# Two interleaved token tiles: the left sides of the sequence transform read as weights with a step of two

## The chip, the cores and the metric

The kernel runs on one core of one Trainium2 chip. The metric is device time in microseconds (us), from runs of the whole program. All data is fp32; the matrix products run on TensorE with operands of the type fp32r, which are split into a high part and a low remainder beforehand, so that three products (high x high, high x low, low x high) stand for one.

## The reference, cut to what matters

The kernel computes a gated sum of a linear-attention block and a Fourier mixing block over 2048 tokens of width 576. The part that the change touches is the last one, the transform along the sequence:

```python
def _B_ref(x, dft_seq_re, dft_seq_im, dft_hid_re, dft_hid_im):
...
    a = jnp.einsum("bsd,ed->bse", x, dft_hid_re)
    b = jnp.einsum("bsd,ed->bse", x, dft_hid_im)
...
    y = jnp.einsum("ts,bse->bte", dft_seq_re, a) - jnp.einsum("ts,bse->bte", dft_seq_im, b)
    return y
...
x = A_x
g = _sigmoid((x * gate_w).sum(-1, keepdims=True))
a = _A_ref(x, A_wqkv, A_wo)
b = _B_ref(x, B_dft_seq_re, B_dft_seq_im, B_dft_hid_re, B_dft_hid_im)
return g * a + (1 - g) * b
```

`dft_seq_re` and `dft_seq_im` are 2048 x 2048, `a` and `b` are 2048 x 576. So two products of 2048 x 2048 by 2048 x 576 are wanted, one for the real and one for the imaginary part.

## The kernel before, in words

The program has these stages, in order of time: the keys of all token tiles, the key-value sums, the queries, the attention output, then for the real part a hidden transform (`Hidden.run`) and a sequence transform (`sequence`), and the same two stages for the imaginary part. A token tile has 128 tokens, so there are 16 of them.

**The product.** Each of the four big products of the Fourier part is done by a 2 x 2 block scheme with seven products instead of eight. For the sequence transform the left matrix (`cr` or `ci`) is cut into four quarters, and the right side (what the hidden transform left in `factors`) likewise. Out of the four quarters of the left side VectorE makes three further sums, so that seven left forms stand side by side. `PRODUCTS` says for each of the seven products which left form `l` meets which right form `f`.

**A batch.** `sequence` walks through `NP * NB` = 32 batches. A batch has one output tile pair (`j`, 8 of them) and one of the four blocks `b` of the contracted tokens. A block holds `BS` = 2 tiles of 128 contracted tokens, numbered by `k`. `Matrix.load` fetches the four quarters of a batch by one DMA on SP's queue into a tile `r` of the shape [128 partitions, 7 forms, 2, 128], forms 3 to 6. `Matrix.make` lets VectorE make forms 0 to 3 from them (L195), ScalarE round all seven to the high part `hi` (L175), and VectorE subtract to get the low part `lo` (L185). All of these operations run over whole rows of the tile and treat its columns alike.

**The matmuls.** Then come 7 products x 2 tiles `k` x 3 passes = 42 matmuls of a batch, each with its own weight load: the left form `c[x][:, l, k]` (128 partitions x 128 columns) is the stationary operand, and `factors[p](y, f)` (128 x 288) is streamed past it into one of seven banks of PSUM. The 128 columns of one left form and one `k` lie next to each other in the tile before. For both sequence transforms together this makes 2 x 32 x 42 = 2688 matmuls and as many loads, all recorded at L1133. After the fourth block of an output tile pair, ScalarE and VectorE empty the banks, mix the rows with the gate and SP's queue stores them.

**What sets the order.** The program order of SP, ScalarE, VectorE and TensorE is written out by hand (`manual_schedule`). Three batches are on their way ahead of the one that is multiplied (`m.load(n + 3)`), and the forms of the next one are made while TensorE works on the present one.

**The host side.** `_layouts` reorders the inputs before the launch. Its function `seq` brings each of the two sequence matrices into the order in which `Matrix.load` reads it: batch by batch, 128 partitions, then four quarters, two tiles `k`, 128 columns.

The two lines around which the change turns are the load of a batch and the use of its tile:

```python
nc.sync.dma_start(out=r[:, 3:7], in_=self.src[j, b])
...
nc.tensor.matmul(ps[q], c[x][:, l, k], factors[p](y, f), ...)
```

Of the kernel before, what the change touches and what calls it, by code (L numbers as in the profile page):

```python
# [14 lines left out]
P = 128  # L15
# [9 lines left out]
NP = NT // 2  # L25
BS = 2
NB = NP // BS
# [26 lines left out]
class Ring:  # L54
# [5 lines left out]
    def next(self):  # L60
        self.n += 1
        return self.at[(self.n - 1) % len(self.at)]
# [71 lines left out]
def kernel(  # L134
# [18 lines left out]
    nc = tc.nc  # L153
# [4 lines left out]
    def at(offset, shape, dtype=F, name="t"):  # L158
        count[0] += 1
        t = nc.alloc_sbuf_tensor_at(f"{name}_{count[0]}", list(shape), dtype,  # L160
                                    offset=base + offset)
        return t.ap()
# [8 lines left out]
    def bank():  # L171
        return psum.tile([P, 512], F, tag="bank", name="bank")
# [17 lines left out]
    def tick():  # L190
        while pending:
            pending.pop(0)()

    def add(dst, a, b, op=ALU.add):
        nc.vector.tensor_tensor(out=dst, in0=a, in1=b, op=op)  # L195
# [11 lines left out]
    def half(h):  # L207
        return slice(h * HALF, (h + 1) * HALF)
# [314 lines left out]
    ps = [[bank()[:, :HALF] for _ in range(2)] for _ in range(FT)]  # L523
# [163 lines left out]
    for c in range(5):  # L687
        ps = [bank(), bank()]
# [223 lines left out]
    factors, backlog = [], []  # L912
# [177 lines left out]

    mix_ring = Ring(MIX_AT, D * 4, 4)

    def sequence(m, g, src, dst, last=None, between=None):
        late, held, stores, rest_lows = [], [], [], []
        for n in range(NP * NB):
            j, b = divmod(n, NB)
            m.load(n + 3)
            if b == 0:
                ps = {k: bank()[:, :HALF] for k in PRODUCTS}
                row = {t: at(mix_ring.next(), [P, D], F, "row") for t in (j, j + NP)}  # L1100
                for t, a in row.items():
                    nc.sync.dma_start(out=a, in_=src[t])
            c = m.ready.pop(0)
            while stores:
                stores.pop(0)()
            if n == 2:
                tick()
                while rest_lows:
                    rest_lows.pop()()
            if m.raws:  # L1110
                new = m.make()
                next(new)
                next(new)
                if b < NB - 1:
                    next(new, None)
            else:
                new = iter(())
                tick()
            if n == 1:
                while backlog:  # L1120
                    backlog.pop(0)()
                rest_lows += pending[-2:]
                del pending[-2:]
            end = last is not None and j == NP - 1
            held.append((b, c))
            if end and b == NB - 2:
                continue
            for q, (l, f) in PRODUCTS.items():
                for b, c in held:
                    for k in range(BS):  # L1130
                        p = b * BS + k
                        for i, (x, y) in enumerate(TURN if n or b else FULL):
                            nc.tensor.matmul(ps[q], c[x][:, l, k], factors[p](y, f),  # L1133
                                             start=(p == 0 and i == 0),
                                             stop=(p == NP - 1 and i == 2))
            held.clear()
            if between is not None:
                between(n)
            while late:
                late.pop(0)()  # L1140
            if b < NB - 1:
                continue
            y = at(Y_AT, [P, 2, 2, HALF], F, "ys")
            c11, c12, c21, c22 = (y[:, i // 2, i % 2] for i in range(4))

            def mix(t, v, h=None, g=g, row=row, store=True, end=end):
                cs = slice(0, D) if h is None else half(h)
                a = row[t][:, cs]
                nc.vector.scalar_tensor_tensor(a, v, g[:, t:t + 1], a, op0=ALU.mult, op1=ALU.add)
                if store:  # L1150
                    stores.append(lambda: nc.sync.dma_start(out=dst[t][:, cs], in_=a))
                if store and end:
                    stores.pop()()

            nc.scalar.activation(c11, ps[1], AF.Copy)
            tick()
            add(c12, ps[6], c11, ALU.subtract)
            add(c11, ps[2], c11)
            next(new, None)
            if end:  # L1160
                mix(j, c11, 0)
                add(c21, c12, ps[7], ALU.subtract)
                add(c12, ps[5], c12)
                add(c22, c12, ps[7], ALU.subtract)
                mix(j + NP, c22, 1)
                mix(j + NP, c21, 0, store=False)
                mix(j, c12, 1, last, store=False)
                mix(j, ps[3], 1)
                mix(j + NP, ps[4], 0, last)
            else:  # L1170
                add(c21, c12, ps[7], ALU.subtract)
                add(c12, ps[5], c12)
                add(c22, c12, ps[7], ALU.subtract)
                add(c12, ps[3], c12, ALU.subtract)
                add(c21, c21, ps[4], ALU.subtract)
                late += [lambda t=t, i=i, y=y, mix=mix: mix(t, y[:, i].rearrange("p a b -> p (a b)"))
                         for i, t in enumerate((j, j + NP))]
        for f in late:
            f()
        for f in stores:  # L1180
            f()
# [11 lines left out]
    for i in range(NT):  # L1193
# [3 lines left out]
        for h in range(2):  # L1197
            ps = bank()
# [62 lines left out]
    mr.load(0)  # L1261
    first.run(mr, {1: 5, 2: 6, 6: 7}, {0: 5, 1: 6, 3: 7})
    sequence(mr, gate_n, att, mid, between=late)
    factors.clear()
    second.run(mi, {1: 5, 2: 6, 6: 7}, {0: 5, 1: 7})
    sequence(mi, gate_m, mid, [out[t * P:(t + 1) * P] for t in range(NT)], last=gate_n)
    paced.close()


def _rows(a):  # L1270

    import numpy as np

    a = np.concatenate([a, a[512:]], axis=0)
    return a.reshape(5, P, a.shape[1]).transpose(1, 0, 2)


def _layouts(inputs):
    import numpy as np

    def seq(c):


        c = c.reshape(2, NP, P, 2, NB, BS, P)
        c = np.stack([c[1, :, :, 0], c[0, :, :, 0], c[1, :, :, 1], c[0, :, :, 1]])
        return c.transpose(1, 3, 5, 0, 4, 2)

    def halves(a):

        a = a.reshape(2, HALF, -1)  # L1290
        return a[:, :2 * P].reshape(2, 2, P, -1), a[:, 2 * P:]

    def left(xt):


        main, rest = halves(xt)
        main = main.reshape(2, 2, P, 2, NP, P)
        rest = rest.reshape(2, 32, 2, 2, 4, P)
        quarters = ((1, 1), (0, 0), (1, 0), (0, 1))
        main = np.stack([main[d, :, :, h] for d, h in quarters])  # L1300
        rest = np.stack([rest[d, :, h] for d, h in quarters])
        main = main.transpose(3, 2, 0, 1, 4).reshape(NP, P, 4, 2 * P)
        rest = rest.transpose(1, 3, 0, 2, 4).reshape(1, P, 4, 2 * P)
        return np.concatenate([main, rest])

    def right(w):

        main, rest = halves(w)
        quarters = ((0, 0), (1, 0), (1, 1), (0, 1))
        cols = (slice(0, HALF), slice(HALF, D))  # L1310
        main = np.stack([main[d][:, :, cols[c]] for d, c in quarters], axis=2)
        rest = np.stack([rest[d][:, cols[c]] for d, c in quarters], axis=1)
        return main, np.concatenate([rest] * 3)

    x = inputs["A_x"][0]
    wr, wr_rest = right(inputs["B_dft_hid_re"].T)
    wi, wi_rest = right(inputs["B_dft_hid_im"].T)
    wqkv, gw = inputs["A_wqkv"], inputs["gate_w"][:, None]
    twice = np.concatenate([x, x[:, KC * P:]], axis=1)
    return {  # L1320
        "xa": _rows(x.T).reshape(P, 5, NT, P).transpose(2, 0, 1, 3),
        "xf": _rows(x.T)[:, :, :FT * P].transpose(1, 0, 2),
        "xg": twice.reshape(NT, P, 5, P).transpose(2, 1, 0, 3),
        "wk": _rows(wqkv[:, D:2 * D]),
        "wq": _rows(np.concatenate([wqkv[:, :D], gw, gw], axis=1)),
        "wv": _rows(wqkv[:, 2 * D:]),
        "wo": inputs["A_wo"],
        "xq": left(x.T),
        "wr": wr,
        "wr_rest": wr_rest,  # L1330
        "wi": wi,
        "wi_rest": wi_rest,
        "cr": seq(inputs["B_dft_seq_re"]),
        "ci": seq(inputs["B_dft_seq_im"]),
    }

# [19 lines left out]
```

## Time and profile before

| | |
|---|---|
| median of 3 runs | 724.67 us (724.57 to 725.0) |
| time of the profiled execution | 725.31 us |
| its span, first to last instruction | 723.6 us |
| granted TensorE clock, mean | 1.000 of full speed |
| mean over the span of what the DMA engines moved | 218 GB/s |

The profile shows one execution of the program. PE stands for the matmuls of TensorE and PEld for its weight loads, which overlap the matmuls; DVE is VectorE, ACT is ScalarE, POOL is GpSimd, SP issues DMAs. A row of a group gives the line of the kernel, the engine, the operation, the tiles written and read with their shapes, how many there are, the time in which at least one of them ran, and the mean duration of one in ns. The profiler models the end of a matmul, so that the durations of successive matmuls overlap; the pace of TensorE is read from the starts.

### The profile page before, as it was taken

To read this page: it belongs to the slowest core of one execution; us is meant where nothing else is said; L and a number is where in the kernel's file an instruction comes from. 1 tells how busy PE (TensorE), PEld (TensorE's weight loads), DVE (VectorE), ACT (ScalarE), POOL (GpSimd) and SP (SyncE) were. 2 spreads that over 40 slices of the span, in tenths; PEclk is the share of its full clock that TensorE was granted. 3 is DMA by queue.
4 is the path that set the end of the run, shared out by engine and by line. 5 is a ranking of instruction groups with operands and counts; after the bars stand their busy time and mean duration, and the time that the engine had idled before them with its cause. 6 is when DMAs were issued, how large, how long until landed. Compare 5 with 4: busy or idle time off the path is not lost.

```text
span 723.6 us, 13786 instructions
## 1 busy us (share of the span) xinstructions
PE 718.9 (99%) x5436; PEld 718.3 (99%) x5436; DVE 594.6 (82%) x954; ACT 331.8 (46%) x519; POOL 54.1 (7%) x94
## 2 busy tenths in 40 slices
PE   9999999999999999999999999999999999999998
PEld 9999999999999999999999999999999999999997
DVE  5699876787999828989999999857889988778884
ACT  5998445678644534453434334223535432342331
POOL 1112200050131100000010000000000000000000
PEclk9999999999999999999999999999999999999999
DMA  7388887874594699544475586889963543454440
GB/s 256 105 286 297 305 304 214 295 223 118 182 358 177 228 321 388 160 153 131 157 249 189 167 289 198 287 313 401 380 214 130 175 143 136 125 179 153 153 154 34
DMA packets 54836, 157.83 MB, mean 218 GB/s; under 512 B 6388, under 2 KB 12084, under 8 KB 53748
## 3 DMA queue, kind: packets, MB, share of 16 engines
q1 hardware_dynamic: 45716, 118.44, 48.5%
q0 software_dynamic: 8768, 38.12, 14.5%
q8 instruction: 43, 0.70, 0.4%
q10 hardware_dynamic: 288, 0.39, 0.2%
q14 instruction: 21, 0.17, 0.1%
HBM read 114.06 MB, written 41.39 MB: 215 GB/s over the span
## 4 chain that ended last, share of the span: by engine, by line
PE 93%; DVE 6%; issue 0%; ACT 0%; DVEq 0%; POOL 0%; POOLq 0%
PE bank L1133 49%; PE bank L205 18%; PE bank L979 14%; PE bank L696 8%; PE bank L532 2%; DVE qs L185 1%; DVE acc L775 1%; DVE pz L767 1%; DVE den L768 1%; PE bank L231 1%; PE bank L678 0%; DVE xb L185 0%; DVE den L772 0%; PE bank L797 0%; DVE xb L195 0%
## 5 line engine op out<-in xcount | busy, mean ns | idle before, releaser
L1133 PE MATMUL bank<-fh,c 128*128 128x288 f32 x1792 | 354.7, 294 | 0.0
L1133 PEld LDWEIGHTS bank<-fh,c 128*128 128x128 f32 x1792 | 286.7, 188 | 0.0
L1133 PE MATMUL bank<-fl,c 128*128 128x288 f32 x896 | 263.6, 294 | 0.0
L175 ACT ACTIVATE c<-craw 128x1792 fp32r<-128x1792 f32 (+1 forms) x84 | 121.3, 1447 | 169.9 <-DVE craw L195 161.2
L1133 PEld LDWEIGHTS bank<-fl,c 128*128 128x128 f32 x896 | 168.7, 188 | 0.0
L185 DVE TENSOR_TENSOR c<-craw,c 128x1792 fp32r<-128x1792 f32 (+4 forms) x86 | 141.9, 1653 | 1.5 <-ACT c L175 1.4
L195 DVE TENSOR_TENSOR craw<-craw 128x256 f32<-128x256 f32 (+1 forms) x192 | 97.9, 512 | 22.0 <-DMA craw<-in_ci_dram 13.6
L205 PE MATMUL bank<-wd,xs 128*128 128x288 f32 (+1 forms) x784 | 105.9, 295 | 0.0
L205 PEld LDWEIGHTS bank<-wd,xs 128*128 128x128 f32 x784 | 104.6, 188 | 0.0
L979 PE MATMUL bank<-wf,xf 128*128 128x288 f32 x588 | 91.1, 295 | 0.0
L979 PEld LDWEIGHTS bank<-wf,xf 128*128 128x128 f32 x588 | 83.4, 189 | 0.0
L205 PE MATMUL bank<-mw,qs 128*128 128x288 f32 x448 | 61.8, 296 | 0.1
L696 PE MATMUL bank<-pk,c 128*128 128x288 f32 x448 | 60.6, 296 | 0.0
L205 PEld LDWEIGHTS bank<-mw,qs 128*128 128x128 f32 x448 | 59.8, 188 | 0.5 <-DVE qs L185 0.4
L696 PEld LDWEIGHTS bank<-pk,c 128*128 128x128 f32 x448 | 59.7, 189 | 0.0
L370 DVE SCALAR_TENSOR_TENSOR acc<-bank,e 128x288 f32<-128x288 f32 x64 | 28.5, 452 | 17.3 <-ACT e L369 17.1
L195 DVE TENSOR_TENSOR ys<-bank,ys 128x288 f32<-128x288 f32 x63 | 28.8, 456 | 16.0 <-PE bank L1133 12.6
L185 DVE TENSOR_TENSOR fl<-fl,fh 128x864 fp32r<-128x864 f32 (+1 forms) x32 | 34.5, 1093 | 6.6 <-ACT fh L175 5.3
L175 ACT ACTIVATE fh<-fl 128x864 fp32r<-128x864 f32 (+1 forms) x32 | 29.8, 950 | 16.6 <-DVE fl L195 16.6
L195 DVE TENSOR_TENSOR fl<-bank,y 128x288 f32<-128x288 f32 x48 | 21.6, 450 | 15.8 <-PE bank L979 15.8
L979 PE MATMUL bank<-wf,xr 96*128 96x288 f32 x112 | 33.3, 298 | 0.0
L195 DVE TENSOR_TENSOR ys<-ys,bank 128x288 f32<-128x288 f32 x47 | 21.2, 450 | 12.4 <-PE bank L1133 11.8
(106 smaller groups left out, 639.6 us busy)
## 6 DMA issues: line engine op xcount, KB each, us to landing
xf<-xm SPq DMA_DIRECT2D x42, 512.0 KB, 8.4
craw<-in_cr_dram SPq DMA_DIRECT2D x32, 512.0 KB, 3.6
craw<-in_ci_dram SPq DMA_DIRECT2D x32, 512.0 KB, 3.7
xm<-xb POOLq DMA_DIRECT2D x8, 1024.0 KB, 5.8
wf<-wm SPq DMA_DIRECT2D x14, 576.0 KB, 6.2
xraw<-in_xa_dram SPq DMA_DIRECT2D x25, 320.0 KB, 3.5
xr<-xr SPq DMA_DIRECT2D x14, 448.0 KB, 8.0
xm<-xb POOLq DMA_DIRECT2D x8, 768.0 KB, 7.4
```

The lines of the kernel that those rows point to most:

```text
L175: return nc.scalar.activation(dst, src, AF.Copy, bias=bias)
L185: nc.vector.tensor_tensor(out=dst, in0=src, in1=hi, op=ALU.subtract)
L195: nc.vector.tensor_tensor(out=dst, in0=a, in1=b, op=op)
L205: nc.tensor.matmul(ps, a, b, start=(n == 0), stop=(n == len(pairs) - 1))
L231: nc.tensor.matmul(warm[:, :P], ones_f, ones_f, start=True, stop=True)
L370: nc.vector.scalar_tensor_tensor(dst, ps, 0.0, e, op0=ALU.max, op1=ALU.add)
L532: nc.tensor.matmul(ps[i][h], x[:, i_x * P:(i_x + 1) * P], wkt.row(h, j), start=(c == 0 and n == 0), stop=(c == KC and n == 1))
L696: nc.tensor.matmul(ps[h][:, :HALF], t[:, a, k], pk[s][:, b, half(h)], start=(s == 0 and n == 0), stop=(s == NT - 1 and n == len(passes) - 1))
L767: nc.vector.scalar_tensor_tensor(pz, acc[2 * k + i], EPS, zb, op0=ALU.add, op1=ALU.mult)
L768: nc.vector.tensor_reduce(out=d[:, i], in_=pz.rearrange("p (h d) -> p h d", d=DH), op=ALU.add, axis=AX.X)
L979: nc.tensor.matmul(ps, a, b, start=(start and n == 0), stop=(n == len(ops) - 1), skip_group_check=True)
L1133: nc.tensor.matmul(ps[q], c[x][:, l, k], factors[p](y, f), start=(p == 0 and i == 0), stop=(p == NP - 1 and i == 2))
```

## The change

The two tiles `k` of a batch are no longer kept one after the other. The host writes their columns in turns: column 0 of tile 0, column 0 of tile 1, column 1 of tile 0, and so on. The tile on the chip keeps its shape and its size; a row of one form still has 256 numbers. A new view `woven` picks the columns of one tile `k` out of such a row, 128 numbers of four bytes that lie eight bytes apart, and the matmul takes it as its stationary operand. DMA, sums, rounding and subtraction are written as before.

```diff
+    def woven(c, l, k):
+        return c[:, l].rearrange("p a b -> p (a b)").rearrange("p (n k) -> p k n", k=BS)[:, k]
+
     def sequence(m, g, src, dst, last=None, between=None):
...
-                            nc.tensor.matmul(ps[q], c[x][:, l, k], factors[p](y, f),
+                            nc.tensor.matmul(ps[q], woven(c[x], l, k), factors[p](y, f),
                                              start=(p == 0 and i == 0),
                                              stop=(p == NP - 1 and i == 2))
...
         c = c.reshape(2, NP, P, 2, NB, BS, P)
         c = np.stack([c[1, :, :, 0], c[0, :, :, 0], c[1, :, :, 1], c[0, :, :, 1]])
-        return c.transpose(1, 3, 5, 0, 4, 2)
+        c = c.transpose(1, 3, 5, 0, 2, 4)
+        return c.reshape(NP, NB, P, 4, BS, P)
```

## The prediction

> **What bounds the kernel now.** I read the page's first and second part, then the end of the chain of waits, then the stages one by one.
>
> ```profile
> span 723.6 us, 13786 instructions
> PE 718.9 (99%) x5436; PEld 718.3 (99%) x5436; DVE 594.6 (82%) x954; ACT 331.8 (46%) x519; POOL 54.1 (7%) x94
> PEclk9999999999999999999999999999999999999999
> PE bank L1133 49%; PE bank L205 18%; PE bank L979 14%; PE bank L696 8%; PE bank L532 2%; DVE qs L185 1%; DVE acc L775 1%; DVE pz L767 1%; DVE den L768 1%; PE bank L231 1%; PE bank L678 0%; DVE xb L185 0%; DVE den L772 0%; PE bank L797 0%; DVE xb L195 0%
> ...
> 313.66 177.16 PE bank L1133 x1344
> 490.82 52.07 PE bank L979 x392
> 542.89 174.03 PE bank L1133 x1320
> 718.41 1.39 DVE row L1149 x3
> ```
>
> TensorE is busy from end to end at a full clock, and the line of the sequence matmuls, L1133, alone is 49% of the chain. In the real sequence transform 1344 matmuls follow one another for 177.16 us, which is 131.8 ns each, with nothing in between; in the imaginary one 1320 of them take 174.03 us, again 131.8 ns. The change touches these matmuls and no others. So the question is what sets 131.8 ns: the streaming of 288 columns, or the weight load.
>
> The groups by form at L1133 can't answer it, since durations of one (294 and 188 ns) overlap:
>
> ```profile
> L1133 PE MATMUL bank<-fh,c 128*128 128x288 f32 x1792 | 354.7, 294 | 0.0
> L1133 PEld LDWEIGHTS bank<-fh,c 128*128 128x128 f32 x1792 | 286.7, 188 | 0.0
> ```
>
> The starts can. The first four rows that follow are weight loads ahead of short matmuls, elsewhere in the kernel, and show how fast loads go when they are what is waited for; the next two are matmuls with only 72 weight columns but 288 streamed ones.
>
> ```profile
> 183.07 0.80 PEld L797 LDWEIGHTS bank<-ident,acc 128*128 128x128 f32 x7
> 183.84 0.14 PEld L798 LDWEIGHTS bank<-ident,last 128*128 128x128 f32 x1
> ...
> 84.14 0.19 PEld L678 LDWEIGHTS bank<-gt,plain 128*126 128x126 f32 x1
> ...
> 84.83 0.14 PEld L678 LDWEIGHTS bank<-gt,plain 128*72 128x72 f32 x1
> ...
> 155.68 0.95 PE L205 MATMUL bank<-plain,kvb 72*72 72x288 f32 x6
> 156.47 0.30 PE L205 MATMUL bank<-wd,xs 128*128 128x288 f32 x1
> ```
>
> Seven loads of 128 columns start within 183.84 - 183.07 = 0.77 us: 110 ns each. Between 84.14 and 84.83 there are six loads of 126 columns (three at L678 and three at L681, in turns): 115 ns each. So a load occupies its path for 110 to 115 ns. With 72 columns of weights the six matmuls take 156.47 - 155.68 = 0.79 us, 132 ns each: with little more than half the weight data to read, the pace is what it is at L1133. The 131.8 ns is therefore the price of streaming 288 columns, and the load lies under it with 131.8 - 110 = 22 ns to spare (17 by the 115).
>
> **The change part by part.** No instruction is added or removed: 2688 loads and 2688 matmuls stay, and so do the DMAs, sums, rounding and subtraction of a batch:
>
> ```profile
> craw<-in_cr_dram SPq DMA_DIRECT2D x32, 512.0 KB, 3.6
> L185 DVE TENSOR_TENSOR c<-craw,c 128x1792 fp32r<-128x1792 f32 x62 | 125.0, 2019 | 1.5 <-ACT c L175 1.4
> L175 ACT ACTIVATE c<-craw 128x1792 fp32r<-128x1792 f32 x64 | 108.9, 1704 | 165.0 <-DVE craw L195 161.2 <-DMA row<-att 3.7
> ```
>
> The DMA of a batch still moves four times 256 numbers per partition in one run of 4 KB; only the host decides which column stands where. VectorE (2019 ns) and ScalarE (1704 ns) go over rows of 1792 numbers without regard to their order. These edits are worth 0 us, without any cover being needed: the same bytes go by the same instructions.
>
> What is left is the load itself: its 128 numbers of four bytes lie eight bytes apart instead of four. By the code, every weight operand of the kernel before has its columns side by side, so no row prices the step, and I bound it.
>
> Lower end of the load: it can't be a gain by itself, since a load that takes less than 110 ns only adds to the 22 ns of spare time. Upper end: the reader has to pass over twice the length, so it takes 2 x 110 = 220 ns, and the pace becomes 220 ns instead of 131.8: 88.2 ns x 2688 = +237 us. Between the two there is a threshold, not a slope: up to 22 ns dearer (a fifth) costs nothing, and each further ns costs 2.7 us (2688 x 1 ns). If a load with a step lost its overlap altogether, 110 ns would be added to each: 2688 x 110 = +296 us, an outer bound that I don't expect, as overlap is a matter of the array and not of the address.
>
> I take the lower end, 0 us. The nearest row is the one of 72 columns: it shows that the amount of weight reading doesn't reach the pace, and a step of two alters just the reading.
>
> The Trainium skill has a rule that bears on this, in "Advanced Engine Details and Errata", section "SBUF Cachelines": the on-chip memory is read in lines of 16 bytes, and a reader keeps full speed as long as at least two accesses in a row fall into a line. Numbers of four bytes at a step of two give exactly two to a line, so by this rule the load keeps its 110 ns and the sum is the same 0 us. The rule leaves no margin, though: a step of two is the widest for four-byte numbers at which two still share a line. No row before the change tests it.
>
> Second unknown: the stream of the 288 columns and the load read the same memory at the same time, and a woven load touches twice as many places. How far such things move the pace, the starts of successive triples show (one low pass, two high passes):
>
> ```profile
> 314.44 0.29 PE L1133 MATMUL bank<-fl,c 128*128 128x288 f32 x1
> 314.56 0.43 PE L1133 MATMUL bank<-fh,c 128*128 128x288 f32 x2
> 314.83 0.30 PE L1133 MATMUL bank<-fl,c 128*128 128x288 f32 x1
> ...
> 318.40 0.31 PE L1133 MATMUL bank<-fl,c 128*128 128x288 f32 x1
> 318.55 0.43 PE L1133 MATMUL bank<-fh,c 128*128 128x288 f32 x2
> 318.82 0.29 PE L1133 MATMUL bank<-fl,c 128*128 128x288 f32 x1
> ```
>
> One triple takes 314.83 - 314.44 = 0.39 us (130 ns a matmul), another 318.82 - 318.40 = 0.42 us (140 ns). All at 130 would be 1.8 ns x 2688 = -5 us; all at 140 would be 8.2 ns x 2688 = +22 us. I take 0 here too: with 72 weight columns the mean was 132 ns, so less weight reading did not help, and I see no reason why more places should hurt.
>
> The sum: 725.31 us of the profiled execution (span 723.6 and 1.7 around it) + 0 = 725.3 us. That execution lies 0.6 us over the median of the runs shown, 724.67, so I put the forecast at 724.8.
>
> VectorE doesn't limit either way. In the real sequence transform it works 156.37 us beside 1352 matmuls, 116 ns for each, below every pace considered here except the far end of the faster rival, which it would just allow (columns: stretch and its length, then busy time and count of PE, PEld, DVE, ACT and POOL, granted clock, DMA share, GB/s):
>
> ```profile
> 313.00:491.00 178.00, 178.00 (x1352) 178.00 (x1352) 156.37 (x217) 64.37 (x46) 6.42 (x9) 1.00 0.65 221
> ```
>
> **The rivals.**
>
> *The load becomes the bound.* Its place is the load at L1133, the price is its time beyond 131.8 ns, and it decides from a load that is a fifth dearer. For it: 22 ns are thin cover, and a load of 110 ns for 128 columns already goes at about one column per 0.86 ns, so any unit that fetches several neighbouring numbers at once would lose by the step. Against it: that very rate looks like one number at a time, for which the step is only an address. At half way between the two ends, 165 ns, the pace rises by 33 ns: +89 us, 814 us. At twice, 962 us. Chance 0.23.
>
> *Collisions.* The load stays within its cover, but the doubled number of places that it touches delays the stream. For it: the triples differ by 10 ns a matmul although they are alike in shape, so something in the addresses does reach the stream. Against it: the 72 columns. Price between triples of 0.41 us and 0.42 us (137 and 140 ns): +13 to +22 us, 738 to 747 us. Chance 0.16.
>
> *Fewer collisions.* The same unevenness could shrink, if the woven load falls into step with the stream. At 130 ns that is -5 us, 720 us. How far it could go at most, the short matmuls show:
>
> ```profile
> 84.14 0.22 PE L681 MATMUL bank<-gt,plain 128*126 128x126 f32 x1
> 84.20 0.33 PE L678 MATMUL bank<-gt,plain 128*126 128x252 f32 x1
> ...
> 84.96 0.20 PE L681 MATMUL bank<-gt,plain 128*72 128x72 f32 x1
> 85.00 1.68 PE L696 MATMUL bank<-pk,c 128*128 128x288 f32 x11
> ```
>
> 126 streamed columns take 0.06 us, 72 take 0.04: 54 columns in 20 ns, an estimate of 0.37 ns each, and so 60 + 162 x 0.37 = 120 ns for 288. All 2688 at 120 ns would be -32 us, 693 us; half way between 130 and 120 is -18 us, 707 us. Against it: nothing shows that the load is what makes the difference between 120 and 131.8, and the 72 columns speak against it. Chance 0.22.
>
> **How the numbers follow.** No change has the remaining 0.39 and is the likeliest case; its own range is 723.3 to 726.3 us. What a measurement of this kernel can tell from no change is about 0.2%, 1.45 us. Faster by more than that: the 0.22 of fewer collisions. Slower: 0.23 + 0.16 plus a little for a load just beyond its cover, 0.41 with what I take from no change, which leaves 0.37. For 8 in 10 the range runs from 707 us, the half-way value of the faster rival, to 815 us, the half-way value of the load-bound one; left out are the dearer half of that rival (0.12) and the far end of the faster one (0.05).
>
> **What would show it.** Right: the two runs of L1133 in the chain stay at 177.2 and about 174 us, starts of loads and matmuls stay 131.8 ns apart, and VectorE and ScalarE keep their means. If the load bounds, the starts of the loads at L1133 lie evenly at more than 132 ns, triples of 0.39 us are gone, the stage takes 1344 times the new load time, VectorE's 156 us stretch over a longer window, and its waits for the banks of L1133 grow, while the stages at L205, L979 and L696 keep 132 ns. If collisions decide, the triples spread wider around a shifted mean. The prediction is wrong if the window of either sequence transform moves by more than 0.7 us.

## The result, and the profile after

The changed kernel takes 729.27 us (median of 3 runs, 729.13 to 729.72) against 724.67 us before: a ratio of 1.0064, 95% interval 1.0041 to 1.0087. It is slower by a little over half a per cent. The profiled execution took 729.13 us, its span is 727.4 us, 3.8 us longer than before.

First three lines of the page of the kernel after: its span, then each engine's busy time, share of the span and number of instructions, then the granted clock in tenths:

```profile
span 727.4 us, 13786 instructions
PE 722.7 (99%) x5436; PEld 722.1 (99%) x5436; DVE 594.8 (82%) x954; ACT 331.6 (46%) x519; POOL 54.0 (7%) x94
PEclk9999999999999999999999999999999999999999
```

The number of instructions is unchanged, TensorE is busy 3.8 us longer, VectorE and ScalarE as long as before. So nothing waits anew; TensorE itself is slower. The end of the chain of waits of the kernel after shows where (start us, length us, engine, tile, line, count; the line is now L1136):

```profile
261.48 51.99 PE bank L979 x392
313.47 179.20 PE bank L1136 x1344
492.67 52.07 PE bank L979 x392
544.74 176.00 PE bank L1136 x1320
```

Each sequence transform is 2.0 us longer (177.16 to 179.20, 174.03 to 176.00), the hidden transforms at L979 are not. 179.20 / 1344 is 133.3 ns a matmul where it was 131.8: 1.5 ns x 2688 = 4.0 us, all of the difference of the two profiled executions (the stages ahead were 0.2 us shorter). The groups at that line, by form:

```profile
L1136 PE MATMUL bank<-fh,c 128*128 128x288 f32 x1792 | 358.7, 296 | 0.0
L1136 PEld LDWEIGHTS bank<-fh,c 128*128 128x128 f32 x1792 | 294.5, 195 | 0.0
L1136 PEld LDWEIGHTS bank<-fl,c 128*128 128x128 f32 x896 | 174.3, 194 | 0.0
```

A load lasts 195 ns in place of 188, idle time stays at 0.0. The triples (one low pass, two high passes) changed too. Two low passes of the kernel after:

```profile
400.11 0.29 PE L1136 MATMUL bank<-fl,c 128*128 128x288 f32 x1
...
400.51 0.30 PE L1136 MATMUL bank<-fl,c 128*128 128x288 f32 x1
```

This triple takes 0.40 us, 133 ns a matmul, and to a hundredth, by the starts in the trace, so do all 892 of them. Before, 259 took 0.39 us, 621 took 0.40 and 12 took 0.41 or 0.42. The woven load has taken away the short triples and the few long ones.

What follows asks why 7 ns more in a load, with some 22 ns of cover, cost 1.5 ns of pace.

### The profile page after: what moved, and what is told of

Its sections match the earlier page's. It is cut to its first block, busy times and chain, and to the rows that moved or that the text cites. A ratio compares the mean times of both kernels' runs of the same rounds, so it can differ in the third digit from the quotient of the medians.

```text
span 727.4 us, 13786 instructions
## 1 busy us (share of the span) xinstructions
PE 722.7 (99%) x5436; PEld 722.1 (99%) x5436; DVE 594.8 (82%) x954; ACT 331.6 (46%) x519; POOL 54.0 (7%) x94
## 4 chain that ended last, share of the span: by engine, by line
PE 93%; DVE 6%; issue 0%; ACT 0%; DVEq 0%; POOL 0%; POOLq 0%
PE bank L1136 49%; PE bank L205 18%; PE bank L979 14%; PE bank L696 8%; PE bank L532 2%; DVE qs L185 1%; DVE acc L775 1%; DVE pz L767 1%; DVE den L768 1%; PE bank L231 1%; PE bank L678 0%; DVE xb L185 0%; DVE den L772 0%; PE bank L797 0%; DVE xb L195 0%
## 5 line engine op out<-in xcount | busy, mean ns | idle before, releaser
L1136 PE MATMUL bank<-fh,c 128*128 128x288 f32 x1792 | 358.7, 296 | 0.0
L1136 PEld LDWEIGHTS bank<-fh,c 128*128 128x128 f32 x1792 | 294.5, 195 | 0.0
L1136 PE MATMUL bank<-fl,c 128*128 128x288 f32 x896 | 266.1, 297 | 0.0
L1136 PEld LDWEIGHTS bank<-fl,c 128*128 128x128 f32 x896 | 174.3, 194 | 0.0
L979 PE MATMUL bank<-wf,xf 128*128 128x288 f32 x588 | 91.1, 295 | 0.0
L979 PEld LDWEIGHTS bank<-wf,xf 128*128 128x128 f32 x588 | 83.4, 189 | 0.0
L979 PE MATMUL bank<-wf,xr 96*128 96x288 f32 x112 | 33.3, 298 | 0.0
```

Of the source, the lines that this page charges most:

```text
L979: nc.tensor.matmul(ps, a, b, start=(start and n == 0), stop=(n == len(ops) - 1), skip_group_check=True)
L1136: nc.tensor.matmul(ps[q], woven(c[x], l, k), factors[p](y, f), start=(p == 0 and i == 0), stop=(p == NP - 1 and i == 2))
```

## The experiments

Three theories stood at the start. **A, collisions**: the load keeps within its cover, but what it reads delays the stream beside it. **B, bound**: the load now outlasts the stream. **C, start**: half of the woven loads begin four bytes off a line, and that is what counts.

**Steps, one by one.** A kernel of TensorE streaks only: 48 matmuls of one kind, one line of source each, with nothing else running. Its core is lines like this one (step 2, 288 columns):

```diff
+    ps = bank(); [nc.tensor.matmul(ps[:128, :288], w[:, 0 + i % 2 * 512 * 2: 0 + i % 2 * 512 * 2 + 255: 2], v[:, 0:288], start=(i == 0), stop=(i == 47)) for i in range(48)]
```

> A kernel of nothing but TensorE streaks of 48 matmuls with their loads, one line for each variant: step of the weights 1, 2, 3, 4, 8; 64, 128, 288 or 512 streamed columns; the streamed operand begun 0, 64, 128 or 192 bytes into a stretch of 256; fewer weight columns. It computes no part of the reference. Theory A (collisions: the load keeps its own time, the stream is delayed by the places that the load touches): with 64 streamed columns, where the load is what is waited for, loads start 110 ns apart at step 1 and at step 2; with 288 columns the pace is about 131 to 132 ns at step 1 and 133.3 at step 2, and steps 4 and 8, which touch more 16-byte lines, go higher. Theory B (the load has become the bound): with 64 columns loads start some 130 ns apart at step 2 and further at step 4, and with 512 columns steps 1 and 2 are equal. Theory C (only the start address of the load counts): the streak with the weights begun 4 bytes later at step 1 shows 133.3 ns.

The chain of waits of this kernel, whose pieces are the streaks (length divided by 48 is the pace). L40 and L41 stream 64 columns at steps 3 and 4, L44 to L47 stream 288 columns at steps 2, 3, 4 and 8, L56 and L57 128 columns at steps 1 and 2, L54 and L55 512 columns at steps 1 and 2, L64 and L65 again 288 columns at steps 1 and 2:

```profile
51.05 10.24 PE bank L40 x48
61.29 11.18 PE bank L41 x48
...
92.02 6.40 PE bank L44 x48
98.42 8.39 PE bank L45 x48
106.81 11.20 PE bank L46 x48
118.00 11.52 PE bank L47 x48
...
167.88 10.90 PE bank L54 x48
178.78 11.20 PE bank L55 x48
189.98 5.31 PE bank L56 x48
195.29 5.66 PE bank L57 x48
...
238.98 6.32 PE bank L64 x48
245.30 6.41 PE bank L65 x48
```

The change is there without the kernel around it: 131.7 ns at step 1 (L64), 133.3 and 133.5 at step 2 (L44, L65). VectorE, DMA and the order of the program are not needed for it. With 128 columns the load is what is waited for: 110.6 ns at step 1, 117.9 at step 2. So the load is 7 ns dearer and still 14 ns short of the stream's pace; theory B is out for step two. With 288 columns the pace is 174.8 ns at step 3 and 233.3 ns at step 4. Theory A's sign is at 512 columns: 227 against 233 ns, though the load ends long before. The streaks of 64 columns can't be set beside these, since TensorE's granted clock fell to half in them, as its row shows:

```profile
PEclk9999995555555999999999999999999999999965
```

They show something else. At half the clock step 4 takes 232.9 ns (L41), the 233.3 ns of the full clock, while step 3 rises from 174.8 to 213.3 ns (L40), and step 2 takes 213.3 ns as well. So the price of step 4 doesn't go with TensorE's clock. Steps 2 and 3 seem to be held there by a price for each column that does, since 213.3 ns is near twice the 110.6 of neighbouring columns.

**The price of further steps in the kernel itself.** The matmul's stationary operand was replaced by a view of the unwoven tile with a step of four, and in another kernel three:

```diff
-                            nc.tensor.matmul(ps[q], c[x][:, l, k], factors[p](y, f),
+                            nc.tensor.matmul(ps[q], picked(c[x], l, k, x), factors[p](y, f),
...
+        s = min(l * 256 + k * 128, 1280)
+        return t[:, s:s + 509:4]
```

> The kernel before, but every weight load of the sequence reads its 128 columns with a step of four from the unwoven tile (other numbers are multiplied, in the same amount). Theory A: one number to a line, 128 lines in place of 64, so at least as much again as step two added: 135 ns a matmul or more, 733 us or more. Theory B: the load alone takes over, 150 ns or more, 775 us or more. Theory C: starts on a line's first byte, as before: 725 us.

> The kernel before with a step of three in every load of the sequence (other numbers are multiplied). A load now touches 96 lines, at 1.82 ns for a line as the step of four shows (233.3 ns for 128 lines): 175 ns, beyond the stream, so the load is the bound: pace 175 ns, 2688 x 43 ns = +116 us, 841 us. [...]

The first piece of the sequence in the two chains, step four first, then step three:

```profile
313.90 313.60 PE bank L1138 x1344
```

```profile
313.26 234.11 PE bank L1138 x1344
```

Step four: 313.60 / 1344 = 233.3 ns, 998.12 us in one run. Step three: 174.2 ns, 838.57 us in one run, as expected (841). Both are loads that outlast the stream, with the same prices as in the streaks. With 128 lines of 16 bytes for step four, 96 for step three and 64 for step two, a line costs 1.82 ns in each case (233.3 / 128, 174.8 / 96, 117.9 / 64 = 1.84): at step two the lines just overtake the 110.6 ns that 128 contiguous columns need. That a step of eight, 32 bytes, costs hardly more than a step of four, 16 bytes (240 ns, L47 above), fits lines of that size.

**Part of the loads, and the start alone.** In one kernel only the low pass reads with a step of two (every third load); in another all loads are contiguous but begin where the woven ones do.

```diff
+        s = l * 256 + (k if x else k * 128)
+        return t[:, s:s + 255:2] if x else t[:, s:s + 128]
```

```diff
+        s = l * 256 + k
+        return t[:, s:s + 128]
```

> The kernel before, but only the loads of the low pass, one in three, read with a step of two from the unwoven tile; the two high passes read contiguous columns (other numbers are multiplied in the low pass). Theory A: a third of the 1.5 ns, 132.3 ns on average, 726 us. Theory B: as A on average, but the added time stands wholly at the matmul whose load has the step. Theory C: half of the low loads begin 4 bytes off, so under a third of the 1.5 ns.

> The kernel before with contiguous loads in the sequence that begin where the woven ones begin: tile 1 four bytes after tile 0 (other numbers are multiplied for tile 1). Theory A: 33 lines in place of 32 for half of the loads, so 131.8 ns and 725 us. Theory B: the same. Theory C: 133.3 ns and 729 us.

The first piece of the sequence in the two chains, low pass first:

```profile
313.88 177.63 PE bank L1138 x1344
```

```profile
312.95 178.21 PE bank L1138 x1344
```

132.2 ns for the low pass (726.35 us in one run), near what A expected, though C's "under a third" fits it as well. But contiguous loads with another start give 132.6 ns (726.63 us), half of the loss with no step at all: A did not allow for that, C only for twice as much. That called for the step without the start:

```diff
+        s = min(l * 256 + k * 128, 1536)
+        return t[:, s:s + 255:2]
```

> The kernel before with every load of the sequence read at a step of two from the unwoven tile, but all of them begun on the first byte of a line (other numbers are multiplied). In the changed kernel half of the loads begin 4 bytes off. Theory A: the step alone makes the pace 133.3 ns, 729 us. Theory C: only the start counts, 131.8 ns, 725 us. Half and half would be 132.5 ns.

```profile
313.25 179.20 PE bank L1138 x1344
544.52 176.00 PE bank L1138 x1320
```

To a hundredth the chain of the changed kernel, 728.89 us in one run. So the step alone is enough for the whole loss, and the start four bytes off adds nothing to it in the woven kernel. Either disturbance costs by itself, and they don't add up.

**Does the loss go with the amount read?** More streaks: 512 columns with other steps and fewer weight columns, other widths, and 288 columns with shifted operands.

> TensorE streaks of 48 matmuls again, nothing of the reference: 512 streamed columns with steps 1, 2, 3, 4, 8 and with fewer weight columns; other widths from 160 to 448 at steps 1 and 2; 288 columns with the weights or the stream begun elsewhere. Theory A (what a load reads delays the stream that runs beside it, by a time that goes with the lines of 16 bytes it touches, far below the point where the load is the bound): at 512 columns, where a load of 118 ns ends long before the stream, step 2 adds 6 to 7 ns to step 1, step 4 at least as much again (240 ns or more), and 32 weight columns take some 10 ns off. Theory B (a load only counts where it outlasts the stream): steps 1, 2 and 3 are equal at 512. Theory C (start addresses): the streak with the weights begun 4 bytes off shows 133.3 ns at 288 columns, those begun on a line's first byte show 131.7 as unshifted.

The chain of this kernel. L38, L39 and L41: 512 columns, steps 1, 2 and 4. L46: 512 columns, step 1, only 32 weight columns. L55 and L56: 256 columns, L57 and L58: 320 columns, each at steps 1 and 2. L67, L71 and L72: 288 columns, step 1, the weights begun 4, 128 and 256 bytes later. L74: 288 columns, step 1, the stream begun 16 bytes later; L78: 128 bytes later; L82: both operands 128 bytes later.

```profile
34.15 10.91 PE bank L38 x48
45.06 11.20 PE bank L39 x48
...
67.56 11.28 PE bank L41 x48
...
123.68 11.12 PE bank L46 x48
...
190.03 5.75 PE bank L55 x48
195.78 5.76 PE bank L56 x48
201.54 7.04 PE bank L57 x48
208.58 7.04 PE bank L58 x48
...
277.30 6.41 PE bank L67 x48
...
302.83 6.40 PE bank L71 x48
309.23 6.32 PE bank L72 x48
...
321.87 6.24 PE bank L74 x48
...
347.18 6.40 PE bank L78 x48
...
376.42 6.33 PE bank L82 x48
```

Theory A's amounts fail. At 512 columns step 4 reads twice the lines of step 2 and adds 2 ns (235.0 against 233.3), not 7, and 32 weight columns, a quarter of the reading, take 231.7 ns, more than the 227.3 of all 128. At 256 and 320 columns step two costs 0.2 ns at most (119.8 and 120.0; 146.7 both), and at 384 and 448 it adds no more than 0.8 ns. And contiguous loads alone go from 130.0 (L74) to 133.3 ns (L78) as the stream's start moves; moving both operands together (L82) brings back 131.9. What counts is how the two readers lie to each other, not how much the load reads. Theory C has its sign, 133.5 ns for a start four bytes off (L67; 134.2 in the first kernel of streaks), but not its reason: a start on a line's first byte 128 bytes later costs 133.3 ns too (L71), and one 256 bytes later 131.7 (L72). That is **theory D**: the distance of the addresses of load and stream sets the pace, and a good distance is worth some ns. That the two fall into a rhythm is the picture behind it, which no run shows directly.

**The kernel's own addresses, shifted.** Streaks of 84 matmuls in the order of a sequence batch, with left and right sides spaced as there, one for each shift of the left sides.

> TensorE streaks of 84 matmuls with the very order and the very addresses of the sequence batch (seven products, two tiles, one low and two high passes), nothing of the reference; one streak for each shift of all left sides against the streamed rows, 0 to 240 bytes in steps of 16, contiguous; four shifts with a step of two; then shifts of 4, 8 and 256 bytes. Theory A (what the load reads delays the stream by an amount of its own): contiguous streaks differ little from shift to shift, 131.8 ns, and all woven ones show 133.3. Theory D (the two readers fall into a rhythm that the distance of their addresses sets): contiguous streaks range from 130 to 133.3 ns as the shift goes, shift 0 gives the 131.8 ns of the kernel before, shift 256 the same again, and 133.3 ns, 320 cycles of a full clock of 2.4 GHz by the skill's page on TensorE, is the ceiling that the woven loads reach and never pass.

Its chain, in part (divide by 84). L50 to L52 and L54: contiguous, shift 0, 16, 32 and 64 bytes. L57, L59, L65: contiguous, 112, 144 and 240. L66 to L69: step two, shift 0, 16, 64 and 128.

```profile
35.49 11.11 PE bank L50 x84
46.60 11.37 PE bank L51 x84
57.96 11.19 PE bank L52 x84
...
80.33 11.13 PE bank L54 x84
...
113.78 11.03 PE bank L57 x84
...
135.98 11.37 PE bank L59 x84
...
203.17 11.04 PE bank L65 x84
214.20 11.20 PE bank L66 x84
225.41 11.21 PE bank L67 x84
236.62 11.21 PE bank L68 x84
247.82 11.18 PE bank L69 x84
```

Contiguous loads range from 131.3 ns (112 bytes) to 135.4 ns (16), and shifts 128 bytes apart give almost the same (16 and 144: 11.37 both; 112 and 240: 11.03 and 11.04). The plain streaks above came back only after 256 bytes; here neighbouring right forms lie 1152 bytes apart, 4.5 times 256, so that a shift of 128 may only exchange their places. That is a reading of the code, not a test. Shift 0, the place in the kernel before, is one of the better ones with 132.3 (the kernel itself has 131.8). The mean of the 16 contiguous shifts is 133.0 ns. With a step of two all four shifts lie between 133.1 and 133.5. D holds in this, except for the ceiling that it named: contiguous loads in a bad place are slower than woven ones.

**The complete kernels, shifted.** If D is right, the contiguous kernel must lose as much as the woven one when its left sides move. Their region is moved by 32 bytes (tiles of earlier stages lie in it too; the hidden transform before the first sequence goes from 51.98 to 52.19 us):

```diff
-SLOT_AT, SLOT = ACC_AT + NT * D * 4 + 256, 7 * BS * P * 4
-Y_AT = SLOT_AT + 7 * SLOT + 512
+SLOT_AT, SLOT = ACC_AT + NT * D * 4 + 256 + 32, 7 * BS * P * 4
+Y_AT = SLOT_AT + 7 * SLOT + 512 - 32
```

> The kernel before, complete and contiguous, with the region of the left sides moved 32 bytes against the streamed rows and nothing else. Theory A (the step itself costs): the sequence keeps 131.8 ns a matmul, 724.7 us. Theory D (the distance of the addresses sets the rhythm): as in the streak with that shift, 1.1 ns more a matmul, 132.9 ns or more, each sequence about 178.6 to 179 us, 727.7 us in all if the other stages keep their pace: the contiguous kernel loses what the woven one lost.

> The same with 64 bytes. Theory A: 131.8 ns. Theory D: back down, 0.3 to 0.4 ns over the kernel before, 132.1 ns, each sequence 177.6 us, 725.6 us if the other stages keep their pace.

> The changed kernel with the region of the left sides moved 32 bytes. Theory D: a woven load covers 1024 bytes and with them every distance in 256, so it has no good or bad place: 133.3 ns and 179.2 us a sequence as unshifted, 729.3 us. Theory A: the same.

The first sequence in the three chains: contiguous and 32 bytes, contiguous and 64, woven and 32.

```profile
314.01 178.92 PE bank L1133 x1344
```

```profile
313.02 178.07 PE bank L1133 x1344
```

```profile
313.64 180.02 PE bank L1136 x1344
```

Contiguous and 32 bytes off: 133.1 ns, 728.95 us (median of 4 runs; ratio to the kernel before 1.0050, interval 1.0033 to 1.0067). 64 bytes off: back to 132.5 ns, 726.65 us in one run. Both are the values of the streaks (133.2 and 132.5), and A's 131.8 is out. D's expectations, taken as differences from shift 0, were lower (132.9 and 132.1), because the kernel starts from 131.8 and the streak from 132.3. The woven kernel 32 bytes off shows 133.9 ns and 730.95 us in one run, 0.6 ns more than D expected: a woven load is not quite indifferent to its place, only more so than a contiguous one. At this place the step still costs 0.8 ns (133.9 against 133.1), half of what it costs unshifted, so the place is not the whole account.

No version that beats the kernel before came of it. The best shift of the streaks, 112 bytes, would be worth 1 ns x 2688 = 2.7 us by their numbers, but the left sides of this kernel fill their slots and begin on multiples of 32 bytes, and a layout for that shift wasn't tried.

## Why the prediction was right and wrong

**The bound was right.** TensorE alone set the time, only the 2688 matmuls of the sequence changed, and DMA, VectorE and ScalarE kept their times to 0.2 us.

**The load's cover was right.** I took 0 for the load as such, because of 22 ns of cover, and it costs 7 ns more (117.9 against 110.6) beneath the stream. The rival in which the load becomes the bound did not come about at step two; steps three and four show it as described, with 838.57 and 998.12 us. The rule of two accesses to a line (the Trainium skill, "Advanced Engine Details and Errata", section "SBUF Cachelines") held in what it said of step two, within those 7 ns. For a different line at each access that section names a penalty without a size; here it goes with the lines, 1.82 ns each. The threshold that I drew, 22 ns for nothing and then each ns in full, is right for 256 and 320 columns, but at 288 a load within its cover came with 1.5 ns.

**The second unknown was the mistake.** "I take 0 here too" was 1.5 ns x 2688 = 4.0 us. The reason given, that 72 weight columns run at the same 132 ns, was sound as a row and wrong as an argument: it shows that the amount of weight reading doesn't matter, and I read it as showing that the weight reading doesn't matter. The streaks say so too: 32 weight columns at step 1 take 131.0 ns. The pace depends on where the two readers lie, and the row with the triples of 0.39 and 0.42 us beside each other, from which I only took bounds, was the visible trace of that.

**The rival that came true** is the one named collisions, with the place right and the size wrong: 4.0 us in the sequences where I had 13 to 22. Its price came from single triples at their slowest; the woven loads don't make every triple a slow one, they take away the short ones and lift the mean to where an ordinary place already has it (133.3 ns; the mean of the 16 contiguous shifts is 133.0). Its sign was that the triples spread wider, and they became even instead, the sign given for the load as the bound, which it was not. Its picture, twice as many places touched, hence more delay, is refuted by the 512 columns. The better description is that the contiguous kernel stood at a good distance and the woven load gave that up; the 0.8 ns that the step still costs at 32 bytes are not explained by it.

**Chances.** No change as the likeliest case was wrong: each sequence moved by 2.0 us where I had named 0.7 us as the point of being wrong. The range of 707 to 815 us held the time, more through the load that might have become the bound than through insight; that was luck. The 120 ns at the far end of the faster rival stood on matmuls of 126 and 72 columns; the fastest streak of 288 columns takes 130.0 ns (L74), and 256 columns already need 119.8.

**What stays open** is why distances act as they do: that the plain streaks come back after 256 bytes, and that 256 and 320 streamed columns feel next to nothing of the step while 288 and 512 do, is measured, not explained.

## What to carry to other kernels

A weight load of four-byte numbers with a step of two was nearly free here, with 14 ns of cover left; from a step of three on it set the pace beside 288 streamed columns, at 1.82 ns for each 16-byte line that it touches. Where TensorE is busy throughout, the distance of stationary and streamed operand within 256 bytes was worth up to 3% of the matmul's pace (131.3 to 135.4 ns here), so a change of layout that moves one of them should be judged against a shifted control before its cause is sought in the change itself. When a row shows that half the amount costs the same, it speaks about amounts and not about places.

## What the runs showed of the hardware that I had not expected

A load beneath a longer stream is hidden without being free of influence: at 512 columns fewer weight columns made the matmuls slower (231.7 ns for 32, 227.3 for 128). TensorE's granted clock fell to half during streaks in which 64 streamed columns waited for loads, and came back with wider streams; the streaks of 128 columns, just as bound by loads, kept the full clock. A step of eight costs hardly more than a step of four, 240 ns against 233 (11.52 us and 11.20 us for 48 matmuls).
